# GpSimd's wide products and subtractions, cut into pieces of 256 or 288 columns

## The chip, the core and the metric

The kernel runs on one core of a Trainium2 chip. Five engines work side by side, each through a queue of its own that it takes in order: TensorE (PE in the profile, its weight loads PEld), VectorE (DVE), ScalarE (ACT), GpSimd (POOL) and SyncE (SP), which here issues the DMAs. They wait for one another by semaphores. The metric is the device time of one execution in microseconds (us).

## The reference

Attention with a top-32 mask, over 8 batches, 8 heads, 576 positions and a head size of 64, and then a gated feed-forward network on its output (4608 rows of 512, inner size 1536), all in float32:

```python
scores = scale * np.matmul(q, k.transpose(0, 1, 3, 2))
kth = np.partition(scores, -top_k, axis=-1)[..., -top_k:-top_k + 1]
scores = np.where(scores >= kth, scores, -1000000000.0)
scores = scores - np.max(scores, axis=-1, keepdims=True)
attn = np.exp(scores)
attn = attn / (np.sum(attn, axis=-1, keepdims=True) + 1e-09)
attn_out = np.matmul(attn, v)
...
gate = 1.0 / (1.0 + np.exp(-(x @ w_gate)))
val = x @ w_val
return (gate * val @ w_out).astype(np.float32)
```

The 32nd largest of each row of 576 scores has to be found exactly, for 8 x 8 x 576 rows.

## The kernel before

**Attention.** A step takes one pair of heads of one batch and 128 query positions; it holds J = 2 score tiles of 128 x 576 (one for each head). The last 64 positions of a batch go in a step with J = 1, both heads sharing one tile. There are 8 x 4 x 5 = 160 steps, 288 tiles in all. The five position blocks of a batch are worked in two groups, blocks 0 and 1, then 2 to 4.

A step goes through three passes, which lie one step apart in program order. `load_queries` (L172) and `load_keys` (L155) bring operands. Each float32 operand is split in a rounded part, made by ScalarE, and the rest, made by GpSimd by a subtraction (L163 for the keys, on 64 of the 128 partitions, 576 columns). `scores` (L180) multiplies on TensorE and ScalarE copies the result to the tile `s` (L202).

`select` (L243) finds the threshold. VectorE takes the 8 largest of each of 8 segments (`cand`, L262) and from them the 8th to the 24th largest in rounds (L266, L268). With a bound a little above the 24th, ScalarE writes the sign of every score against the bound to `under`, in bfloat16, and counts (L274, one instruction for each tile). GpSimd then writes u = s x under for both tiles (L277), VectorE takes the 8 largest of u (`below`, L281, one for each tile), and L282 picks the wanted one into `kths`. Meanwhile ScalarE forms the exponentials `e` (L209). In `masked` (L211) VectorE multiplies e by the mask s >= kth and sums (L214, inputs `s` and `e`); GpSimd and VectorE form the reciprocal (L217, L218, L220). In the pass after, `turn` transposes `e` on TensorE (L301) and `weigh` multiplies it by the values; GpSimd writes the rest of that product too (`xl`, L344).

**Feed-forward.** `ffn` (L346) is a generator: for each group of 256 or 320 rows it makes three products for each weight tile (L377 to L379), the gate (L382 to L385, GpSimd writes `gl` in L385) and three products with the second weights (L397 to L399), summed up by GpSimd (L405). `run` (L410) draws pieces of it between the steps of attention, some 384 rows behind.

**Weights.** `split_weight` (L115) takes each of 18 weight blocks, in two halves of 512 columns, from its float64 words to two float32 parts. VectorE works on the bit patterns (L138 to L140), GpSimd multiplies `frac` by `lead` (L142), TensorE adds the parts up (L145 to L147). Nine blocks are split during the first group's steps, the others at their first use, all in the first 336 us of the profile.

**What sets the order.** The instructions are written in program order, and the framework lays down each engine's queue and the semaphores by a planner that forecasts the time of every instruction (`schedule_with_timeline_sim=True`). At run time each engine follows its own queue in order. Dependencies go by the part of a tile that an instruction reads or writes.

Of the kernel before, what the change touches and what calls it, by code (L numbers as in the profile page):

```python
# [10 lines left out]
F32 = mybir.dt.float32  # L11
# [5 lines left out]
ALU = mybir.AluOpType  # L17
# [11 lines left out]
def tile_topk_attention_then_gated_ffn(  # L29
# [8 lines left out]
    nc = tc.nc  # L38
    P = 128
    B, H, _, S = k.shape  # L40
    D = P // 2
    HALF = S // 2
# [72 lines left out]
    def split_weight(idx, held):  # L115

        if held:
            wt = pools["w"].tile([P, 2, 2, NP, P], F32R, tag="w", name=f"wsplit_{idx}")
            ready[idx] = wt
        for i in range(2):
            raw = pre_pools["raw"].tile([P, NP * P, 2], U32, tag="raw", name=f"wraw_{idx}_{i}")
            half = slice(i * NP * P, (i + 1) * NP * P)
            nc.sync.dma_start(raw.rearrange("p n t -> p (n t)"), w[idx][:, half].bitcast(U32))
            low, top = raw[:, :, 0], raw[:, :, 1]
            if held:
                pair = wt[:, i].rearrange("p a c n -> p a (c n)")  # L130
            else:
                pair = pre_pools["parts"].tile([P, 2, NP * P], F32R, tag="pair", name=f"wpair_{idx}_{i}")
            lead = pre_pools["parts"].tile([P, NP * P], F32, tag="lead", name=f"wt_lead_{idx}_{i}")
            rest = ps_f.tile([P, NP * P], F32, tag="f", name=f"wrest_{idx}_{i}")
            frac = pre_pools["parts"].tile([P, NP * P], F32R, tag="frac", name=f"wt_frac_{idx}_{i}")
            lead_u = lead.bitcast(U32)
            nc.scalar.activation(lead, top.bitcast(F32), AF.Copy, scale=2.0**-112)
            nc.vector.tensor_scalar(lead_u, lead_u, 3, None, op0=ALU.logical_shift_left)  # L138
            nc.vector.scalar_tensor_tensor(top, top, 0x80000000, lead_u, op0=ALU.bitwise_and, op1=ALU.bitwise_or)
            nc.vector.tensor_scalar(lead_u, top, 0xFF800000, None, op0=ALU.bitwise_and)  # L140
            nc.scalar.activation(frac, low, AF.Copy)
            nc.gpsimd.tensor_tensor(frac, frac.bitcast(F32), lead, op=ALU.mult)  # L142
            bits = top.bitcast(F32)
            nc.scalar.activation(pair[:, 0], bits, AF.Copy)
            nc.tensor.matmul(rest, ident, bits, start=True, stop=False)  # L145
            nc.tensor.matmul(rest, minus, pair[:, 0], start=False, stop=False)
            nc.tensor.matmul(rest, plus, frac, start=False, stop=True)  # L147
            nc.scalar.activation(pair[:, 1], rest, AF.Copy)
            nc.sync.dma_start(w_split[idx][:, i], pair.bitcast(F32))
# [5 lines left out]
    def load_keys(b, p, nm):  # L155

        ks = []
        for h in (2 * p, 2 * p + 1):
            raw = bkr.tile([P, S], F32, tag="kraw", name=f"kraw_{nm}_{h}")
            nc.sync.dma_start(raw, k[b, h])  # L160
            kt = bk.tile([P, S], F32R, tag="k", name=f"k_{nm}_{h}")
            nc.scalar.activation(kt, raw, AF.Copy)
            nc.gpsimd.tensor_tensor(kt[D:], raw[D:], kt[D:], op=ALU.subtract)  # L163
            ks.append(kt)
        return ks

# [40 lines left out]
    def numerators(J, s, st, e):  # L207
        for j in range(J):
            nc.scalar.activation(e[:, j], s[:, j], AF.Exp, bias=st[:, j : j + 1], scale=1.0 / SHRINK)  # L209

    def masked(J, s, kth, st, e, nm):  # L211

        for j in range(J):
            nc.vector.scalar_tensor_tensor(  # L214
                e[:, j], s[:, j], kth[j], e[:, j], op0=ALU.is_ge, op1=ALU.mult, accum_out=st[:, 4 + j : 5 + j]
            )
        nc.gpsimd.tensor_scalar(st[:, 4 : 4 + J], st[:, 4 : 4 + J], 1e-9, None, op0=ALU.add)  # L217
        nc.vector.reciprocal(st[:, 6 : 6 + J], st[:, 4 : 4 + J])  # L218
        inv = bi.tile([P, P], F32, tag="inv", name=f"inv_{nm}")
        nc.gpsimd.tensor_copy(  # L220
            inv.rearrange("p (j d) -> p j d", j=J), st[:, 6 : 6 + J].unsqueeze(2).to_broadcast([P, J, P // J])
        )
        return e, inv
# [19 lines left out]
    def select(J, s, col, nm):  # L243

        cand = b2.tile([P, 2, NSEG * 8], F32, tag="cand", name=f"cand_{nm}")
        tops = b2.tile([P, 2, 16], F32, tag="tops", name=f"tops_{nm}")
        below = b2.tile([P, 2, 8], F32, tag="below", name=f"below_{nm}")
        st = bi.tile([P, 8], F32, tag="st", name=f"st_{nm}")
        sums = bi.tile([P, 2], F32, tag="sums", name=f"sums_{nm}")
        pick = b2.tile([P, 2, 8], F32, tag="pick", name=f"pick_{nm}")
        e = b3.tile([P, 2, S], F32, tag="e", name=f"e_{nm}")
        u = b2.tile([P, 2, S], F32, tag="u", name=f"u_{nm}")
        under = b2.tile([P, 2, S], BF16, tag="under", name=f"under_{nm}")
        for j in range(J):  # L260
            for g in range(NSEG):
                nc.vector.max(cand[:, j, 8 * g : 8 * g + 8], s[:, j, g * SEG : (g + 1) * SEG])  # L262
        for r in range(LEAD // 8):
            for j in range(J):
                t = tops[:, j, 8 * r : 8 * r + 8] if r < 2 else leads[:, n_tiles - col - j : n_tiles - col - j + 8]
                nc.vector.max(t, cand[:, j])  # L266
                if r < LEAD // 8 - 1:
                    nc.vector.match_replace(cand[:, j], t, cand[:, j], LOWEST)  # L268
            if r == 0:
                nc.gpsimd.tensor_scalar(st[:, 0:J], tops[:, :J, 0], -1.0 / SHRINK, None, op0=ALU.mult)  # L270
        for j in range(J):
            at = 2 * (n_tiles - col - j + 7) + 1
            bound = leads.bitcast(BF16)[:, at : at + 1]
            nc.scalar.activation(  # L274
                under[:, j], s[:, j], AF.Sign, bias=bound, scale=-CUT, accum_out=sums[:, j : j + 1]
            )
        nc.gpsimd.tensor_tensor(u[:, :J], s[:, :J], under[:, :J], op=ALU.mult)  # L277
        numerators(J, s, st, e)
        yield
        for j in range(J):  # L280
            nc.vector.max(below[:, j], u[:, j])  # L281
            nc.vector.scalar_tensor_tensor(  # L282
                pick[:, j],
                wanted,
                sums[:, j : j + 1],
                below[:, j],
                op0=ALU.is_equal,
                op1=ALU.mult,
                accum_out=kths[:, col + j : col + j + 1],
            )  # L290
        yield masked(J, s, [kths[:, col + j : col + j + 1] for j in range(J)], st, e, nm)
# [54 lines left out]
    def ffn(nm0, xs, t0, rows, general):  # L346
# [5 lines left out]
        def load(idx):  # L352
            if idx in ready:
                return ready.pop(idx)
            if not (general or idx in stored):
                split_weight(idx, True)
                stored.add(idx)
                return ready.pop(idx)
            wt = pools["w"].tile([P, 2, 2, NP, P], F32R, tag="w", name=f"w_{nm0}_{idx}")
            nc.sync.dma_start(wt.rearrange("p i a c n -> p i a (c n)").bitcast(F32), w_split[idx])  # L360
            return wt
# [48 lines left out]
    def run(general):  # L410
# [32 lines left out]
        for n in range(len(steps) + 2):  # L443
            if n < len(steps):
                g, p, i = steps[n]
                b, first, end = groups[g]
                m = n

                if not general and g == 0:
                    k = m * (HELD + LOADED) // (2 * NP)  # L450
                    for t in range(k, (m + 1) * (HELD + LOADED) // (2 * NP)):
                        split_weight(order[t], t < HELD)
                        stored.add(order[t])
                fetch(n + FETCH)
                ask(n + ASK)
                begin(n + AHEAD)
                J = 2 if i < NT else 1
                nm = f"{mark}{b}_{i}_{p}"
                if general:
                    parts[n] = select_any(J, staged.pop(n), nm)  # L460
                else:
                    parts[n] = select(J, staged.pop(n), col, nm)
                next(parts[n])
                col += J
# [104 lines left out]
```

## Time and profile before

| | |
|---|---|
| median of 3 runs | 1672.96 us (1672.12 to 1673.5) |
| the profiled execution's own time | 1670.51 us |
| its span | 1668.7 us |
| mean granted TensorE clock | 0.978 of full speed |
| busy: PE, DVE, ACT, POOL | 1559.4, 1383.5, 1179.0, 1103.6 us |
| GpSimd: u of two tiles (L277) | 128 instructions of 128 x 1152 |
| GpSimd: u of one tile (L277) | 32 instructions of 128 x 576 |
| GpSimd: k (L163) | 64 instructions of 64 x 576 |
| GpSimd: frac (L142) | 36 instructions of 128 x 512 |

The profile shows one execution. A row of a group reads: line, engine, operation, output <- inputs, shapes, count | busy us, mean ns of one | idle us of the engine just before them, and what ended it. A row of a wait reads: who <- whom, us in all, times, the longest. In the rows of a timeline stand start and length in us. An instruction's length is from its start on the engine to its end, so what it waits for after its semaphores are there is inside it.

### The profile page before, as it was taken

The numbers are of one execution on the slowest core, as the hardware profiler recorded it, in microseconds if no ns is written. First come the engines' busy times: TensorE is split into PE (matmuls) and PEld (weight loads), VectorE is DVE, ScalarE is ACT, GpSimd is POOL, SyncE is SP. The second block draws the span as 40 slices with busy tenths as digits, with TensorE's granted clock in tenths as the row PEclk, the third lists the DMA queues.
The fourth block names the chain that finished last, engine by engine and source line by source line (L and its number), as shares of the span: only waits on it lengthen the run. The fifth ranks groups of instructions, "written<-read, shape, count | busy, mean of one in ns | idle before, by whom it ended". The sixth has DMA issues, their size and how long they took to land.

```text
span 1668.7 us, 37046 instructions
## 1 busy us (share of the span) xinstructions
PE 1559.4 (93%) x11666; PEld 1415.2 (85%) x11666; DVE 1383.5 (83%) x6353; ACT 1179.0 (71%) x2739; POOL 1103.6 (66%) x1331
## 2 busy tenths in 40 slices
PE   5678878899999999999999999999999999999998
PEld 2347756798999989999898989998898989999898
DVE  6999999968998889988989789988989789988310
ACT  7787878756777777766777677766777677766422
POOL 7667776866776767677666767677666767666323
PEclk8779999999999999999999999999999999999999
DMA  7556555777777677677686677677686677666686
GB/s 239 188 170 225 169 180 184 265 273 238 252 264 250 230 277 263 230 256 261 220 294 229 238 266 263 231 248 268 219 295 227 239 253 263 230 231 219 247 322 219
DMA packets 101006, 402.01 MB, mean 241 GB/s; under 512 B 11200, under 2 KB 39872, under 8 KB 65472
## 3 DMA queue, kind: packets, MB, share of 16 engines
q1 hardware_dynamic: 100800, 399.55, 68.7%
q8 instruction: 94, 1.54, 0.4%
q14 instruction: 112, 0.92, 0.2%
HBM read 371.20 MB, written 28.31 MB: 239 GB/s over the span
## 4 chain that ended last, share of the span: by engine, by line
PE 40%; DVE 24%; ACT 8%; POOL 5%; issue 3%; DMA 2%; POOLq 0%; ACTq 0%
DVE e L214 6%; PE pz L377 6%; PE pz L378 6%; PE pz L379 6%; DVE cand L262 6%; DVE below L281 4%; PE pss L195 4%; PE po L320 3%; POOL u L277 3%; PE po L397 3%; PE po L398 3%; PE po L399 3%; PE pt L301 2%; DVE pick L282 2%; ACT e L209 2%
## 5 line engine op out<-in xcount | busy, mean ns | idle before, releaser
L377 PE MATMUL pz<-xh,w 128*128 128x320 f32 (+1 forms) x1472 | 444.2, 302 | 4.4 <-DVE gf L383 2.4
L379 PE MATMUL pz<-xh,w 128*128 128x320 f32 (+1 forms) x1472 | 438.5, 298 | 0.0
L378 PE MATMUL pz<-xl,w 128*128 128x320 f32 (+1 forms) x1472 | 438.2, 298 | 0.0
L277 POOL TENSOR_TENSOR u<-s,under 128x1152 f32<-128x1152 f32 (+1 forms) x160 | 356.2, 2229 | 71.3 <-ACT under L274 54.7
L262 DVE MAX8 cand<-s 128x8 f32<-128x72 f32 x2304 | 350.5, 216 | 38.9 <-ACT s L202 38.2
L214 DVE SCALAR_TENSOR_TENSOR e<-s,kths,e 128x576 f32<-128x576 f32 x288 | 305.8, 1075 | 37.3 <-ACT e L209 37.1
L274 ACT ACTIVATE under<-s,leads 128x576 bf16<-128x576 f32 x288 | 223.3, 776 | 118.4 <-DVE leads L266 107.8
L377 PEld LDWEIGHTS pz<-xh,w 128*128 128x128 f32 x1472 | 278.7, 189 | 6.9 <-ACT gf L382 3.0
L378 PEld LDWEIGHTS pz<-xl,w 128*128 128x128 f32 x1472 | 278.9, 189 | 0.0
L379 PEld LDWEIGHTS pz<-xh,w 128*128 128x128 f32 x1472 | 278.7, 189 | 0.0
L385 POOL TENSOR_TENSOR gl<-gf,gh 128x256 fp32r<-128x256 f32 (+1 forms) x192 | 166.6, 868 | 129.0 <-ACT gh L384 126.2
L281 DVE MAX8 below<-u 128x8 f32<-128x576 f32 x288 | 205.9, 747 | 54.6 <-POOL u L277 54.4
L195 PE MATMUL pss<-k,qh 128*128 128x288 f32 (+2 forms) x672 | 204.3, 321 | 22.6 <-ACT s L202 15.5
L398 PE MATMUL po<-gl,w 128*128 128x320 f32 (+1 forms) x736 | 218.2, 301 | 0.0
L397 PE MATMUL po<-gh,w 128*128 128x320 f32 (+1 forms) x736 | 214.5, 307 | 2.6 <-ACT part L404 1.3
L399 PE MATMUL po<-gh,w 128*128 128x320 f32 (+1 forms) x736 | 215.5, 298 | 0.0
L302 ACT ACTIVATE et<-pt 128x384 f32<-128x384 f32 x384 | 181.3, 490 | 47.9 <-PE pt L301 46.8
L301 PE MATMUL pt<-ident,e 128*128 128x128 f32 x1152 | 184.2, 279 | 28.9 <-DVE e L214 24.2
L209 ACT ACTIVATE e<-s,st 128x576 f32<-128x576 f32 x288 | 209.4, 775 | 2.1 <-POOL st L270 2.1
L202 ACT ACTIVATE s<-pss 128x576 f32<-128x576 f32 x288 | 186.5, 648 | 3.3 <-PE pss L195 2.2
L195 PE MATMUL pss<-k,ql 128*128 128x288 f32 (+2 forms) x672 | 187.0, 299 | 0.3 <-POOL ql L177 0.3
L301 PEld LDWEIGHTS pt<-ident,e 128*128 128x128 f32 x1152 | 142.2, 143 | 42.5 <-DVE e L214 19.2
(102 smaller groups left out, 3543.7 us busy)
## 6 DMA issues: line engine op xcount, KB each, us to landing
w<-ws SPq DMA_DIRECT2D x276, 1024.0 KB, 5.2
v<-in_v_dram SPq DMA_DIRECT2D x64, 352.0 KB, 4.1
qraw<-in_q_dram SPq DMA_DIRECT2D x160, 128.0 KB, 3.6
kraw<-in_k_dram SPq DMA_DIRECT2D x64, 288.0 KB, 3.8
wraw<-in_w_dram SPq DMA_DIRECT2D x36, 512.0 KB, 4.0
ws<-wsplit SPq DMA_DIRECT2D x24, 512.0 KB, 4.4
ws<-wpair SPq DMA_DIRECT2D x12, 512.0 KB, 3.8
out_dram<-acc SPq DMA_DIRECT2D x32, 160.0 KB, 4.8
```

The lines of the kernel that those rows point to most:

```text
L195: nc.tensor.matmul(ps[:, half, o : o + n], x[:, h * P : (h + 1) * P], ks[h][:, k0 : k0 + n], start=t == 0, stop=t == len(todo) - 1,)
L214: nc.vector.scalar_tensor_tensor(e[:, j], s[:, j], kth[j], e[:, j], op0=ALU.is_ge, op1=ALU.mult, accum_out=st[:, 4 + j : 5 + j])
L262: nc.vector.max(cand[:, j, 8 * g : 8 * g + 8], s[:, j, g * SEG : (g + 1) * SEG])
L277: nc.gpsimd.tensor_tensor(u[:, :J], s[:, :J], under[:, :J], op=ALU.mult)
L281: nc.vector.max(below[:, j], u[:, j])
L301: nc.tensor.transpose(pt[:, c], ef[:, k0 : k0 + P], ident)
L377: nc.tensor.matmul(ps, wt[:, u, 0, d], xh[:, cols], start=d == 0, stop=False)
L378: nc.tensor.matmul(ps, wt[:, u, 0, d], xl[:, cols], start=False, stop=False)
L379: nc.tensor.matmul(ps, wt[:, u, 1, d], xh[:, cols], start=False, stop=d == NP - 1)
L397: nc.tensor.matmul(ps, wt[:, e % 2, 0, f], gh, start=f == 0, stop=False)
L398: nc.tensor.matmul(ps, wt[:, e % 2, 0, f], gl, start=False, stop=False)
L399: nc.tensor.matmul(ps, wt[:, e % 2, 1, f], gh, start=False, stop=f == FG - 1)
```

## The change

Three GpSimd lines are cut along the columns. `frac` goes in two pieces of 256 columns, the keys' rest in two of 288, and u in two pieces of 288 for each tile, so four instructions in place of one where J = 2. The pieces of u stand in order of the tile; each reads one half of one tile of `s` and `under`. Every product and difference is the same as before, and nothing else is changed.

```diff
@@ split_weight
-            nc.gpsimd.tensor_tensor(frac, frac.bitcast(F32), lead, op=ALU.mult)
+            for c in (slice(0, 2 * P), slice(2 * P, 4 * P)):
+                nc.gpsimd.tensor_tensor(frac[:, c], frac[:, c].bitcast(F32), lead[:, c], op=ALU.mult)
@@ load_keys
-            nc.gpsimd.tensor_tensor(kt[D:], raw[D:], kt[D:], op=ALU.subtract)
+            for c in (slice(0, HALF), slice(HALF, S)):
+                nc.gpsimd.tensor_tensor(kt[D:, c], raw[D:, c], kt[D:, c], op=ALU.subtract)
@@ select
-        nc.gpsimd.tensor_tensor(u[:, :J], s[:, :J], under[:, :J], op=ALU.mult)
+        for j in range(J):
+            for half in range(2):
+                c = slice(half * HALF, (half + 1) * HALF)
+                nc.gpsimd.tensor_tensor(u[:, j, c], s[:, j, c], under[:, j, c], op=ALU.mult)
```

## The prediction

> **What bounds the kernel now.** I read the page's totals and the chain of waits first, then the busy time by stretches, and after that who waits for whom in the stretches that stand out.
>
> ```profile
> span 1668.7 us, 37046 instructions
> PE 1559.4 (93%) x11666; PEld 1415.2 (85%) x11666; DVE 1383.5 (83%) x6353; ACT 1179.0 (71%) x2739; POOL 1103.6 (66%) x1331
> PE 40%; DVE 24%; ACT 8%; POOL 5%; issue 3%; DMA 2%; POOLq 0%; ACTq 0%
> DVE e L214 6%; PE pz L377 6%; PE pz L378 6%; PE pz L379 6%; DVE cand L262 6%; DVE below L281 4%; PE pss L195 4%; PE po L320 3%; POOL u L277 3%; PE po L397 3%; PE po L398 3%; PE po L399 3%; PE pt L301 2%; DVE pick L282 2%; ACT e L209 2%
> 0.00:84.00 84.00, 47.13 (x164) 28.94 (x165) 69.55 (x289) 66.71 (x133) 56.26 (x66) 0.79 0.64 212
> 84.00:336.00 252.00, 208.16 (x1336) 164.37 (x1335) 247.65 (x1033) 203.24 (x449) 181.53 (x196) 0.93 0.60 200
> 336.00:1540.00 1204.00, 1183.61 (x9259) 1106.40 (x9258) 1039.93 (x4938) 867.63 (x2056) 826.98 (x1016) 1.00 0.71 249
> ```
>
> A row of stretches gives the length, then busy us of PE, PEld, DVE, ACT and POOL. There are two regimes. From 84 to 336 DVE is busy 247.65 of 252 us (98%) and PE 208.16 (83%): VectorE sets the pace while the weights are split. From 336 to 1540 PE is busy 1183.61 of 1204 us, so at most 20.4 us are to be had there by feeding PE better, and DVE (86%) has room. Who PE waits for before 336 says the same:
>
> ```profile
> PE wrest L145 <- DVE wraw L139: 25.8, 12, 6.9
> PE pt L301 <- DVE e L214: 24.2, 10, 4.7
> ```
>
> **How GpSimd enters.** No row shows PE waiting long for GpSimd. It enters through VectorE, as this stretch does, one row for each instruction (start us, length us):
>
> ```profile
> 898.60 1.44 POOL L163 TENSOR_TENSOR k<-kraw,k 64x576 fp32r<-64x576 f32 x1
> 900.11 2.78 POOL L277 TENSOR_TENSOR u<-s,under 128x1152 f32<-128x1152 f32 x1
> ...
> 898.64 2.01 DVE L214 SCALAR_TENSOR_TENSOR e<-s,kths,e 128x576 f32<-128x576 f32 x1
> 900.72 2.79 DVE L214 SCALAR_TENSOR_TENSOR e<-s,kths,e 128x576 f32<-128x576 f32 x1
> ```
>
> The same instruction can take 0.79 us (row of L214 below). Here the first one starts 0.04 us after k and ends at 900.65, that is 0.61 after k's end; taking off its own 0.79, it was let go 0.18 us before k ended. The second starts during u and ends at 903.51, again 0.62 after u's end at 902.89. So this DVE instruction stands inside its own row until the running GpSimd instruction is nearly over. Between k and u the first DVE instruction got its turn, although u started 0.07 us after k; u paid with 2.78 us. Minimum, median and maximum of the lines whose rows spread like that:
>
> ```profile
> L214 DVE SCALAR_TENSOR_TENSOR e<-s,kths,e x288: 790/814/2927, 27.0 to 1554.2; 128x576 f32<-128x576 f32 x144
> L282 DVE SCALAR_TENSOR_TENSOR pick<-wanted,sums,below x288: 198/222/2404, 25.5 to 1553.8; 128x8 f32<-128x8 f32 x144
> L139 DVE SCALAR_TENSOR_TENSOR wraw<-wraw,wt_lead x36: 665/683/2916, 11.0 to 302.7; 128x512 uint32<-128x512 uint32 x36
> L138 DVE TENSOR_SCALAR wt_lead<-wt_lead x36: 397/415/1951, 10.5 to 301.3; 128x512 uint32<-128x512 uint32 x36
> L140 DVE TENSOR_SCALAR wt_lead<-wraw x36: 400/416/1758, 12.1 to 305.2; 128x512 uint32<-128x512 uint32 x36
> ```
>
> Their means before 336 us (ns, ahead of the last bar):
>
> ```profile
> L214 DVE SCALAR_TENSOR_TENSOR e<-s,kths,e 128x576 f32<-128x576 f32 x55 | 55.2, 1021 | 0.0
> L139 DVE SCALAR_TENSOR_TENSOR wraw<-wraw,wt_lead 128x512 uint32<-128x512 uint32 x36 | 38.1, 1058 | 0.0
> L282 DVE SCALAR_TENSOR_TENSOR pick<-wanted,sums,below 128x8 f32<-128x8 f32 x56 | 32.1, 592 | 0.0
> L138 DVE TENSOR_SCALAR wt_lead<-wt_lead 128x512 uint32<-128x512 uint32 x36 | 22.7, 631 | 11.4 <-ACT wt_lead L137 11.3
> L140 DVE TENSOR_SCALAR wt_lead<-wraw 128x512 uint32<-128x512 uint32 x36 | 19.5, 541 | 0.0
> ```
>
> Mean less minimum, times the count, before 336: L214 55 x 0.231 = 12.7; L282 56 x 0.394 = 22.1; L139 36 x 0.393 = 14.1; L138 36 x 0.234 = 8.4; L140 36 x 0.141 = 5.1. That is 62.4 us of standing still in the stage that VectorE bounds. Set against the GpSimd instruction that runs then, one by one, 42 of these stalls with 44.9 us lie behind the three lines that the change cuts: u 19 with 29.5 us, k 9 with 6.8, frac 14 with 8.6. The first and the last of the 42:
>
> ```profile
> 12.93 1.24 DVE L138 TENSOR_SCALAR wt_lead<-wt_lead 128x512 uint32<-128x512 uint32 x1
> ...
> 333.10 1.31 DVE L282 SCALAR_TENSOR_TENSOR pick<-wanted,sums,below 128x8 f32<-128x8 f32 x1
> ```
>
> **The change, part by part.** *GpSimd's own time.* These are the means by shape:
>
> ```profile
> L277 POOL TENSOR_TENSOR u<-s,under 128x1152 f32<-128x1152 f32 x128 | 312.5, 2445 | 57.0 <-ACT under L274 45.2 <-DMA w<-ws 2.6 <-ACT et L302 2.6
> L163 POOL TENSOR_TENSOR k<-kraw,k 64x576 fp32r<-64x576 f32 x64 | 97.1, 1518 | 23.3 <-issue 8.0 <-PE pss L195 3.9 <-DMA kraw<-in_k_dram 3.4
> L385 POOL TENSOR_TENSOR gl<-gf,gh 128x320 fp32r<-128x320 f32 x96 | 87.4, 911 | 85.8 <-ACT gh L384 85.0
> L385 POOL TENSOR_TENSOR gl<-gf,gh 128x256 fp32r<-128x256 f32 x96 | 79.1, 824 | 43.2 <-ACT gh L384 41.2 <-PE pt L301 0.6
> L142 POOL TENSOR_TENSOR wt_frac<-wt_frac,wt_lead 128x512 fp32r<-128x512 f32 x36 | 48.9, 1359 | 14.8 <-DVE wt_lead L140 11.0 <-DVE pick L282 1.4 <-DVE tops L266 1.1
> L277 POOL TENSOR_TENSOR u<-s,under 128x576 f32<-128x576 f32 x32 | 43.8, 1367 | 14.3 <-ACT under L274 9.4 <-PE pss L195 4.0 <-DMA w<-ws 0.6
> ```
>
> No row has 288 columns. The line through the two u rows (1367 at 576, 2445 at 1152) gives 289 ns + 1.87 ns a column, so 828 ns for 288 and 768 for 256; the 256 and 320 rows give 868 between them, and 824 for 256. The first pair is the lower bound, the second the upper, and I take the upper, as its shapes are nearest. u of two tiles: 4 x 868 - 2445 = +1.03 us, 128 times, 131 us (lower bound 111). u of one: 2 x 868 - 1367 = +0.37, 32 times, 12 (9). k: 2 x 868 - 1518 = +0.22, 64 times, 14 (9). frac: 2 x 824 - 1359 = +0.29, 36 times, 10 (6). Together +167 us (136), so GpSimd goes from 66% to 76%. Before 336 it is 31 u (25 of two tiles, by the 128 to 32 of the whole), 18 k and 36 frac: 26 + 2 + 4 + 10 = 42 us on top of 56.26 + 181.53, or 280 of 336 us, 83%. GpSimd does not become the bound in either regime, so I cost this part at nothing; its cover is VectorE's queue before 336 and PE's after it.
>
> *VectorE's stalls before 336.* A piece holds VectorE up for its length less 0.18, about 0.62 to 0.69 us, against 2.2 for u. If a DVE instruction arrives at any moment of a piece, it waits 0.31 to 0.34: 42 x 0.33 = 14 us remain and 31 are saved. That is the upper bound, for there is a row that speaks for more meetings:
>
> ```profile
> 332.23 0.94 DVE L282 SCALAR_TENSOR_TENSOR pick<-wanted,sums,below 128x8 f32<-128x8 f32 x1
> ...
> 332.25 0.90 POOL L385 TENSOR_TENSOR gl<-gf,gh 128x320 fp32r<-128x320 f32 x1
> 333.10 1.28 POOL L277 TENSOR_TENSOR u<-s,under 128x576 f32<-128x576 f32 x1
> ```
>
> This pick stood behind gl, and the next one (333.10, above) behind the u that followed. With pieces each DVE instruction of a pair can meet one. If all do, the second waits a piece less the 0.16 us that it needs to arrive, about 0.48: 42 x (0.33 + 0.48) = 34 us remain and 11 are saved. I take 21, half way, since L214 and L282 do come in pairs, and L138 to L140 do not. Saved DVE time becomes time where DVE is full, which is 252 of the 336 us: 21 x 0.75 = 16 us, bounds 8 and 23. Against it stands a u that ends later, which would delay L281; before 336 L281 waits for u only three times, so I take off 2: -14 us.
>
> *After 336.* Stalls shrink there as well, but PE is full, so the gain is at most the 20.4 us that PE idles. A row that speaks for some of it:
>
> ```profile
> 466.22 0.78 ACT L274 ACTIVATE under<-s,leads 128x576 bf16<-128x576 f32 x1 [2.79 <-DVE leads L266]
> 469.30 2.39 POOL L277 TENSOR_TENSOR u<-s,under 128x1152 f32<-128x1152 f32 x1 [0.21 <-ACT xh L343]
> ```
>
> The first tile's sign was ready at 467.00, and u began at 469.30, because the one instruction needs both tiles. Pieces of the first tile could start up to 2.3 us earlier, and the first L281 with them. Against it: all four end about 1 us later once they run, and what is behind them in GpSimd's queue (gl for PE's second product, acc for ACT, ql and k for the next scores) comes that much later. Bounds -20 and +15, the latter being a u longer by 1.0 us at the places where u stands on the chain (3% of 1668.7 is 50 us, some 20 of them at 2.4), less a little. I take -3.
>
> Sum, against the profiled execution's 1670.5 us: -14 - 3 gives 1653.5; the median of the runs shown, 1672.96, is 2.5 above that execution, so 1656.
>
> **The rivals.** *PE takes back its idle time too (0.12):* the earlier start of the first tile's pieces ends ACT's and PE's small waits after 336; -14 - 18 gives 1641. For it: the 2.3 us above. Against it: PE's waits there are spread over many causes.
>
> *No difference (0.13):* the pairs meet two pieces each, 11 us saved, 8 of them on the path, and the later ends of u take 8 back after 336: 1673. For it: the pair at 332.23. Against it: u's stalls are long and few, and a wait that is cut in four seldom doubles.
>
> *Slower, through u itself (0.17):* every DVE turn that falls between two pieces also holds u up, as 2.78 against a mean of 2445 ns shows (+0.3). With two turns u ends 1.0 + 0.6 us later, and L281 waits for it in order, with L262 and L214 queued behind it:
>
> ```profile
> DVE below L281 <- POOL u L277: 51.9, 47, 2.9
> ```
>
> These 47 waits of 336 to 1540 would grow by 1.6 us, 75 us of DVE's 164 idle; at the 20 places on the chain it is 32 us. Less 14 before 336 it gives 1673 + 18 = 1691, and 1675 at half as many places. It decides from the point where the later end outweighs the earlier start.
>
> *Slower, because VectorE gets no turn between the pieces (0.05):* then a stall lasts to the end of the last piece, and stalls grow with the square of the length: u (3.47 / 2.445) squared is 2.0, +30 us before 336; k and frac +2 and +4; times 0.75, +27, so 1700. The row at 898.64 speaks against it: VectorE got in between k and u. The Trainium skill, GPSIMD Engine Reference, section Instruction dispatch, says that consecutive Pool instructions are no barrier: each of the eight cores goes on to the next one as soon as its own share is done. By that rule the engine might never be free between two pieces; this trace, with the turn taken at 900.04, does not bear it out.
>
> **How the numbers follow.** The forecast, 1656, has 0.53; its own range, from 23 saved and 6 more after 336 down to 8 saved and 4 lost, is 1644 to 1669. About 0.2% (3.3 us) is what a measurement of this kernel tells from no change. Faster: 0.53 + 0.12 = 0.65. Same: 0.13. Slower: 0.17 + 0.05 = 0.22. The range takes in the first rival and most of the slower one: 1638 to 1686. What no row prices is the planner: it lays down each engine's order from its own forecast of times, and other durations can reorder any queue.
>
> **What would show it.** In the profile after: L214, L282 and L139 with maxima near 1.5 us instead of 2.9 and means closer to their minima; DVE busy about 1320 instead of 1383 us; GpSimd 1240 to 1270 us with pieces of 0.8 to 0.9; the DVE-bound stage over some 14 us sooner. It is wrong if DVE's stalls keep their sum while their number doubles, if L281's wait for u grows past 80 us, or if PE shows idle stretches after 336 with GpSimd ahead of them.

## The result, and the profile after

The changed kernel takes 1640.03 us (median of 6 runs, 1639.24 to 1640.95), the kernel before 1672.16 beside it. The ratio is 0.9813, with a 95% interval of 0.9803 to 0.9824: 32 us faster, where 17 were forecast.

The totals of the changed kernel's page with its chain of waits, and its busy time by stretches (length, then busy us of PE, PEld, DVE, ACT and POOL; the stretches are cut where the same stages end):

```profile
span 1637.9 us, 37664 instructions
PE 1560.0 (95%) x11666; PEld 1418.4 (87%) x11666; DVE 1363.1 (83%) x6353; ACT 1182.3 (72%) x2739; POOL 1200.0 (73%) x1847
PE 68%; DVE 14%; POOL 5%; ACT 3%; DMA 2%; issue 2%; POOLq 0%; ACTq 0%; SPq 0%; DVEq 0%
```

```profile
0.00:84.00 84.00, 52.41 (x188) 30.69 (x188) 71.72 (x288) 68.62 (x138) 67.67 (x104) 0.83 0.69 223
84.00:330.00 246.00, 210.17 (x1317) 165.16 (x1316) 235.97 (x1035) 203.91 (x447) 208.87 (x298) 0.91 0.59 199
330.00:1510.00 1180.00, 1176.64 (x9247) 1106.23 (x9246) 1031.07 (x4944) 868.54 (x2056) 884.87 (x1392) 1.00 0.72 255
1510.00:1638.00 128.00, 120.76 (x920) 116.32 (x918) 24.29 (x88) 41.18 (x101) 38.56 (x56) 0.99 0.73 264
```

PE's busy time is the same (1560.0 us, 1559.4 before), so the gain is PE's idle time. Before it was idle 80.7 us up to 336, 20.4 from there to 1540 and 8.2 after; now, up to 330, to 1510 and after, 67.4, 3.4 and 7.1. The splitting stage gave 13.3 us and the long middle stage 17.0. The chain of waits shows it too: DVE's share falls from 24% to 14%, and PE's rises from 40% to 68%.

The three cut lines and two of the lines that stood behind them (minimum, median and maximum in the last rows):

```profile
L282 POOL TENSOR_TENSOR u<-s,under 128x288 f32<-128x288 f32 x576 | 443.5, 792 | 104.8 <-ACT under L276 92.4 <-PE po L333 2.0 <-PE po L404 1.0
L165 POOL TENSOR_TENSOR k<-kraw,k 64x288 fp32r<-64x288 f32 x128 | 111.0, 887 | 18.8 <-POOL u L282 7.9 <-ACT k L163 3.5 <-issue 2.6
L143 POOL TENSOR_TENSOR wt_frac<-wt_frac,wt_lead 128x256 fp32r<-128x256 f32 x72 | 60.4, 858 | 14.8 <-DVE wt_lead L140 6.7 <-DVE cand L264 3.8 <-DVE tops L268 2.9
```

```profile
L216 DVE SCALAR_TENSOR_TENSOR e<-s,kths,e x288: 792/819/1509, 27.7 to 1524.9; 128x576 f32<-128x576 f32 x144
L287 DVE SCALAR_TENSOR_TENSOR pick<-wanted,sums,below x288: 197/352/835, 26.0 to 1524.5; 128x8 f32<-128x8 f32 x144
L139 DVE SCALAR_TENSOR_TENSOR wraw<-wraw,wt_lead x36: 666/892/1245, 9.9 to 297.9; 128x512 uint32<-128x512 uint32 x36
```

(L216 and L287 are L214 and L282 of before.) The longest stalls are gone: L216's maximum is 1.51 us instead of 2.93, that of the pick 0.84 instead of 2.40. But the medians of the pick and of L139 rose, from 222 to 352 and from 683 to 892 ns: stalls are shorter and more frequent.

Below, a *stall* is what L214, L282 and L138 to L140 take above their undisturbed 0.796, 0.208, 0.404, 0.670 and 0.404 us, summed over all of them; shorter ones count as nothing. These lengths are those that the shortest fifth of each line's rows stays under before. It is 178 us before and 133 in the changed kernel.

### The profile page after: what moved, and what is told of

Read it like the earlier page. It is cut to its first block, busy times and chain, and to the rows that moved or that the text cites. A ratio compares the mean times of both kernels' runs of the same rounds, so it can differ in the third digit from the quotient of the medians.

```text
span 1637.9 us, 37664 instructions
## 1 busy us (share of the span) xinstructions
PE 1560.0 (95%) x11666; PEld 1418.4 (87%) x11666; DVE 1363.1 (83%) x6353; ACT 1182.3 (72%) x2739; POOL 1200.0 (73%) x1847
## 4 chain that ended last, share of the span: by engine, by line
PE 68%; DVE 14%; POOL 5%; ACT 3%; DMA 2%; issue 2%; POOLq 0%; ACTq 0%; SPq 0%; DVEq 0%
PE pz L382 11%; PE pz L383 11%; PE pz L384 11%; PE pss L197 7%; PE po L402 5%; PE pt L306 5%; PE po L403 5%; PE po L404 5%; PE po L325 5%; DVE cand L264 3%; DVE e L216 3%; DVE below L286 2%; PE po L327 2%; DMA w<-ws 1%; POOL u L282 1%
## 5 line engine op out<-in xcount | busy, mean ns | idle before, releaser
L282 POOL TENSOR_TENSOR u<-s,under 128x288 f32<-128x288 f32 x576 | 443.5, 792 | 104.8 <-ACT under L276 92.4
L383 PE MATMUL pz<-xl,w 128*128 128x320 f32 (+1 forms) x1472 | 437.1, 297 | 0.0
L264 DVE MAX8 cand<-s 128x8 f32<-128x72 f32 x2304 | 345.1, 216 | 28.7 <-ACT s L204 27.7
L276 ACT ACTIVATE under<-s,leads 128x576 bf16<-128x576 f32 x288 | 224.4, 779 | 116.8 <-DVE leads L268 104.4
L216 DVE SCALAR_TENSOR_TENSOR e<-s,kths,e 128x576 f32<-128x576 f32 x288 | 274.0, 957 | 9.8 <-ACT e L211 7.9
L383 PEld LDWEIGHTS pz<-xl,w 128*128 128x128 f32 x1472 | 279.0, 190 | 0.1
L286 DVE MAX8 below<-u 128x8 f32<-128x576 f32 x288 | 216.6, 752 | 58.1 <-POOL u L282 56.4
L306 PE MATMUL pt<-ident,e 128*128 128x128 f32 x1152 | 179.6, 279 | 13.3 <-DVE e L216 10.3
```

The source lines that it names most:

```text
L216: nc.vector.scalar_tensor_tensor(e[:, j], s[:, j], kth[j], e[:, j], op0=ALU.is_ge, op1=ALU.mult, accum_out=st[:, 4 + j : 5 + j])
L282: nc.gpsimd.tensor_tensor(u[:, j, c], s[:, j, c], under[:, j, c], op=ALU.mult)
L306: nc.tensor.transpose(pt[:, c], ef[:, k0 : k0 + P], ident)
L383: nc.tensor.matmul(ps, wt[:, u, 0, d], xl[:, cols], start=False, stop=False)
```

## The experiments

All ratios are against runs of the kernel before on the same chip. There are three theories of the gain. *Stalls*: shorter pieces hold VectorE for less time. *Early start*: the first tile's pieces can start before the second tile's sign is there. *Planner*: it forecasts other times for the pieces and lays the queues in another order. The programs show that it does: of the instructions that run (a fall-back path does not), 24% of TensorE's stand elsewhere than before, 32% of VectorE's, 38% of ScalarE's and 29% of GpSimd's other than the cut ones (all that are not in the longest common order).

**Which part, and which property of it.** The edits are written out as loops here; the runs have the same pieces. First u alone.

```diff
-        nc.gpsimd.tensor_tensor(u[:, :J], s[:, :J], under[:, :J], op=ALU.mult)
+        for j in range(J):
+            for c in (slice(0, 288), slice(288, 576)):
+                nc.gpsimd.tensor_tensor(u[:, j, c], s[:, j, c], under[:, j, c], op=ALU.mult)
```

> Only u is cut (four pieces of 288 for two tiles, two for one); k and frac stay whole. Three theories of the 32 us. Stalls: the gain is VectorE standing for less time behind GpSimd, and u has 80 of the 113 us that lay behind the three cut lines before: about 1648 us. Early start: the gain is that pieces of the first tile run before the second tile's sign is there, which only u has: about 1640. Planner: the gain is another order of the queues: no value follows, anything from 1640 to 1680.

Measured: 1635.49 us, ratio 0.9778 (0.9761 to 0.9794). That is the whole gain, and by the ratios 0.35% more than the change; the planner laid an order of its own for this kernel too. Then k and frac alone, as the change has them:

```diff
-            nc.gpsimd.tensor_tensor(frac, frac.bitcast(F32), lead, op=ALU.mult)
+            for c in (slice(0, 2 * P), slice(2 * P, 4 * P)):
+                nc.gpsimd.tensor_tensor(frac[:, c], frac[:, c].bitcast(F32), lead[:, c], op=ALU.mult)
-            nc.gpsimd.tensor_tensor(kt[D:], raw[D:], kt[D:], op=ALU.subtract)
+            for c in (slice(0, HALF), slice(HALF, S)):
+                nc.gpsimd.tensor_tensor(kt[D:, c], raw[D:, c], kt[D:, c], op=ALU.subtract)
```

> Only k and frac are cut in two; u stays one instruction. Stalls: 33 of the 113 us lay behind k and frac, and half of the saving is in the stage that VectorE bounds: about 1662 us. Early start: nothing of it is in k and frac: 1672. Planner: no value follows; a time below 1655 or above 1680 would speak for it.

Measured: 1663.65 us, 0.9951 (0.9935 to 0.9968), as the stalls had it, though this order too is another than before. The two parts do not add up: 37 and 8 us alone, 32 together.

u by tile only, 576 columns each:

```diff
-        nc.gpsimd.tensor_tensor(u[:, :J], s[:, :J], under[:, :J], op=ALU.mult)
+        for j in range(J):
+            nc.gpsimd.tensor_tensor(u[:, j], s[:, j], under[:, j], op=ALU.mult)
```

> u is cut by tile alone: one instruction of 576 columns for each tile (about 1.29 us), k and frac stay whole. Stalls: VectorE is held up to 1.1 us instead of 2.2, so half of u's stall saving: about 1660 us. Early start: nearly all of the gain of u_only, within 4 us of it, about 1642. Planner: no relation.

Measured: 1669.33 us, 0.9984 (0.9975 to 0.9994). Pieces that can start early bring next to nothing in the order laid for them, and both forecasts, 1660 and 1642, were missed. Stalls rose, to 201 us, though each piece can hold VectorE for 1.1 us only, which the stall theory did not have.

Short pieces that cannot start early, for they cross both tiles:

```diff
-        nc.gpsimd.tensor_tensor(u[:, :J], s[:, :J], under[:, :J], op=ALU.mult)
+        for c in range(0, S, 288 // J):
+            w = slice(c, c + 288 // J)
+            nc.gpsimd.tensor_tensor(u[:, :J, w], s[:, :J, w], under[:, :J, w], op=ALU.mult)
```

> u is cut in four pieces of 144 columns of both tiles (288 elements each, as long as those of the change), so that every piece needs both signs and none can start early; with one tile two pieces of 288. k and frac stay whole. Stalls: as u_only, about 1648 us. Early start: no gain, and a u that ends 1 us later: 1672 to 1680. Planner: no relation.

Measured: 1643.86 us, 0.9838 (0.9822 to 0.9854). Most of the gain comes without the early start, so that theory is out as its main cause; whether it has a part in the 0.6% by which u alone is faster is not shown. Short pieces and a new order are still together here.

**Order and length, taken apart.** The planner's forecast depends on how many pieces there are and on their columns in all, so pieces of other widths can leave its order as it is. In the next two kernels every instruction stands at the same place as in its counterpart, on every engine, but for three pairs of neighbours that are swapped in the first of them. First the change itself with long pieces:

```diff
-            for half in range(2):
-                c = slice(half * HALF, (half + 1) * HALF)
+            for c in (slice(0, 8), slice(8, S)):
```

> The change with the pieces of u at other places: for each tile 8 columns and then 568, in place of 288 and 288; k and frac in two pieces as in the change. All queues then hold the same instructions in the same order as the changed kernel; only GpSimd's two long pieces hold VectorE for about 1.1 us instead of 0.62. Stalls: most of u's gain goes, about 1660 us. Planner: the order is that of the change, so 1640, within 4 us. Early start: the same as the change, 1640.

Measured: 1645.68 us, 0.9845 (0.9828 to 0.9863), 5 us or 0.3% slower than the change. The forecast of the stall theory, 1660, was wrong: halving the hold from 1.1 to 0.62 us is worth some 5 us in this order. The cost of the pieces is no reason, as these rows of GpSimd show (0.24 + 1.31 us against 2 x 0.79):

```profile
L277 POOL TENSOR_TENSOR u<-s,under 128x568 f32<-128x568 f32 x288 | 377.9, 1312 | 0.1
...
L277 POOL TENSOR_TENSOR u<-s,under 128x8 f32<-128x8 f32 x288 | 69.7, 242 | 105.0 <-ACT under L274 95.0 <-PE po L328 2.0 <-DMA w<-ws 0.3
```

Then the pieces across both tiles, with a last one about as long as the u of before:

```diff
-        for c in range(0, S, 288 // J):
-            w = slice(c, c + 288 // J)
+        for w in (slice(0, 8), slice(8, 16), slice(16, 24), slice(24, S)):   # J = 1: 0 to 8, 8 to S
```

> The counterpart: the queues of the run with four pieces of both tiles (144 columns of each), every instruction at the same place, but the pieces are 8, 8, 8 and 552 columns of both tiles, so the last holds VectorE for nearly as long as the u of before (about 2.1 us). Stalls: back to 1665 or more. Planner: within 5 us of the 1643.9 of the even pieces.

Measured: 1670.55 us, 1.0000 (0.9991 to 1.0009). All of the gain is gone in the very order that had it. So this order alone brings no time; long holds undo it. The stalls are 177 us, as before the change (129 with the even pieces).

Now the other way round: the queues of before as they were laid, and u cut afterwards at its place (the edit in words):

```diff
+    # after the planner: each u in GpSimd's queue becomes 4 instructions of 288 columns (2 for one tile);
+    # the first waits for what u waited for, the last signals what u signalled
```

> The kernel before with its queues exactly as the planner laid them for it, and each u then replaced, at its place, by four pieces of 288 columns (two for one tile); the first piece waits for what u waited for, the last one signals. No other instruction stands elsewhere. Stalls: the pieces alone bring the gain of u, about 1645 us. Planner: the pieces alone bring nothing, and GpSimd's added 0.8 us for each u costs a little: 1670 to 1680. Both in parts: between.

Measured: 1677.39 us, 1.0036 (1.0022 to 1.0049): slower. So the pieces alone do not bring the gain either. The profile says why. First the two stalled lines of this run as groups (mean ns ahead of the last bar), then VectorE's waits in it (us in all, times, longest):

```profile
L214 DVE SCALAR_TENSOR_TENSOR e<-s,kths,e 128x576 f32<-128x576 f32 x288 | 290.3, 1022 | 41.5 <-ACT e L209 41.3
L282 DVE SCALAR_TENSOR_TENSOR pick<-wanted,sums,below 128x8 f32<-128x8 f32 x288 | 111.0, 400 | 0.3
```

```profile
DVE below L281 <- POOL u L277: 91.4, 87, 3.3
...
DVE e L214 <- ACT e L209: 41.3, 31, 4.0
```

The same waits of the kernel before, and then of the changed one:

```profile
DVE below L281 <- POOL u L277: 54.4, 50, 2.9
...
DVE e L214 <- ACT e L209: 37.1, 28, 4.0
```

```profile
DVE below L286 <- POOL u L282: 56.4, 91, 2.1
...
DVE e L216 <- ACT e L211: 7.9, 19, 0.9
```

In the old order the pieces cut VectorE's stalls from 178 to 139 us, and its wait for u grew from 54 to 91: what one gives the other takes. In the order of the change the wait for u does not grow, though its pieces are as long, and that for `e` nearly goes.

One more thing differs between this run and the change: in the old order the first piece waits for both signs and only the last one signals, while in the change each L286 needs the pieces of its own tile alone. The first L286 of a step with two tiles starts before the last piece has ended in 127 of 128 steps of the change, and in none of this run. The run with the crossing pieces settles that this is not what the gain needs: there too no L281 starts before the last piece, there are as many pieces of as many elements, and k and frac are whole. Only the order differs, and it stands at 0.9838 against 1.0036, with a wait for u of 55 us against 91.

With k and frac cut in place too:

```diff
+    # as above, and each k and each frac becomes two instructions of half the columns
```

> As the run before it, with k and frac replaced in place by two pieces each as well, so that GpSimd does exactly the pieces of the change in the order of before. Stalls: about 1640 us, the time of the change. Planner: 1670 to 1685.

Measured: 1686.26 us, 1.0087 (1.0073 to 1.0101). GpSimd does all the pieces of the change here, and the kernel is 46 us slower than the change. VectorE waits 105 us for u.

Last, half as many pieces in the old order (in words again, against the run with four):

```diff
-    # each u of two tiles becomes 4 instructions of 288 columns
+    # each u of two tiles becomes 2 instructions of 576 columns; u of one tile stays whole
```

> The queues of before once more, with each u of two tiles replaced in place by two pieces of 576 columns; u of one tile stays whole. The four pieces in this order cut VectorE's stalls by 38 us and made its wait for u 30 us longer. If the one is given back by the other, two pieces, which hold VectorE for 1.1 instead of 2.2 us and make u only 0.2 us longer, should keep part of the gain: stalls down by some 20 us, the wait for u up by less than 10, and 1660 to 1668 us. If VectorE's stalls do not count in this order whatever u does: 1672 to 1677.

Measured: 1671.42 us, 0.9996 (0.9987 to 1.0005), no difference. The value expected from half the stalls, 1660 to 1668, was missed, and the time lies just below the other, 1672 to 1677: stalls fell by 8 us and not by 20, and the wait for u rose by 12 to 66.3.

**The queues in program order, and more pieces.** The two kernels with the planner's forecast switched off, which keeps their orders more alike (of the instructions that run, 2% of TensorE's, 16% of VectorE's, 7% of ScalarE's and 4% of GpSimd's uncut ones stand elsewhere; the shares in the expectation count a fall-back path too, which does not run):

```diff
-    with tile.TileContext(nc, schedule_with_timeline_sim=True) as tc:
+    with tile.TileContext(nc, schedule_with_timeline_sim=False) as tc:
```

> The kernel before, with the planner laying the queues by the program's order instead of by forecast times. It only serves as the base of the next run; some per cent slower or faster than 1672 us, no theory says which.

> The changed kernel, its queues laid by the program's order as in the run before it; the two have nearly the same order on every engine (1% of TensorE's instructions, 10% of VectorE's and GpSimd's stand elsewhere). Stalls: 1 to 2% faster than its base. Planner: within 0.3% of its base.

Measured: 1929.68 and 1949.36 us, 1.1545 and 1.1669 of the kernel before, so the pieces cost 1.1% there. Both forecasts, 1 to 2% faster and within 0.3%, were missed. The stalls are 78 us in the first and 74 in the second: there was little to save in that order, and VectorE's wait for `e` rose from 19 to 55 us. That the pieces cost time fits the run in the old order, though this regime, where VectorE waits some 300 us for u in both, is far from the kernel's.

u alone, in pieces of 144 columns:

```diff
-            for c in (slice(0, 288), slice(288, 576)):
+            for c in (slice(0, 144), slice(144, 288), slice(288, 432), slice(432, 576)):
```

> u in pieces of 144 columns, eight for two tiles and four for one; k and frac whole. Stalls alone: each piece holds VectorE for some 0.3 us instead of 0.62, so the stalls behind u halve again; PE is nearly full already, so 1630 to 1636 us against 1635.5 of the four pieces. If GpSimd's own time decides by then (each piece has a fixed part, so u of two tiles takes about 4 us instead of 3.2): above 1645.

Measured: 1647.1 us, 0.9840 (0.9823 to 0.9856), by the ratios 0.6% or 10 us behind the pieces of 288, where 1630 to 1636 was the forecast of the stalls alone. Stalls fall further, to 127 us, but u of two tiles now takes 8 x 0.52 = 4.2 us, and the wait for it is 77 us. That is the other forecast, above 1645: GpSimd's time decides by then, and the wait for u is where it shows.

**All of them in one table.** us, from each profiled execution; VectorE's waits are those for u (L281) and for `e` (L214).

| kernel | ratio | stalls | wait for u | wait for e | sum | span |
|---|---|---|---|---|---|---|
| before | 1 | 178 | 54 | 37 | 270 | 1668.7 |
| the change | 0.9813 | 133 | 56 | 8 | 197 | 1637.9 |
| u alone | 0.9778 | 141 | 53 | 10 | 204 | 1635.7 |
| u, crossing pieces | 0.9838 | 129 | 55 | 17 | 201 | 1641.4 |
| the change, 8 + 568 | 0.9845 | 140 | 53 | 9 | 202 | 1642.5 |
| u, 144 columns | 0.9840 | 127 | 77 | 15 | 219 | 1645.7 |
| k and frac alone | 0.9951 | 163 | 52 | 25 | 241 | 1662.0 |
| crossing, 8 + 8 + 8 + 552 | 1.0000 | 177 | 52 | 14 | 242 | 1667.8 |
| u by tile | 0.9984 | 201 | 55 | 8 | 264 | 1667.0 |
| old order, u in 2 | 0.9996 | 170 | 66 | 36 | 272 | 1670.3 |
| old order, u in 4 | 1.0036 | 139 | 91 | 41 | 272 | 1679.0 |
| old order, all pieces | 1.0087 | 134 | 105 | 42 | 281 | 1684.4 |
| program order, before | 1.1545 | 78 | 307 | 19 | 403 | 1925.5 |
| program order, the change | 1.1669 | 74 | 289 | 55 | 418 | 1944.9 |

Stalls alone do not order these kernels (139 us stands at 1679.0 and 140 at 1642.5). The sum of the three nearly does: five kernels with 197 to 219 us lie between 1636 and 1646, the next seven, with 241 to 281, between 1662 and 1684, and the two in program order, with 403 and 418, far behind. Inside the seven it tells less: 242 and 270 stand at nearly the same time. It is lost time of VectorE, whether it stands in an instruction or ahead of one. VectorE has the same work in all of these kernels, so the sum is in part bookkeeping: it tells where the time went, and the runs with the order held tell why.

## Why the prediction was right or wrong

**The direction and the number.** 1656 was forecast and 1640 measured, inside the range; the rival "PE takes back its idle time too", at 1641 with a chance of 0.12, gave the number. Its reason, the early start, is not what the gain needs (0.9838 without it), so its number was in good part luck. The 2.3 us that it rested on were not free either: from 467.65 to 469.08 GpSimd worked on ql and gl, so in the order of before no piece could have started much sooner.

**Before 336: -14 forecast, 13.3 measured, by a poorer way than the one worked out.** The step took 21 us of stalls off. Up to 336 all stalls went from 61 to 49 us, 12 us. Those behind the three cut lines went only from 44.9 to 39.7, in 108 places instead of 42. The pairs met more pieces than even the lower bound (11 us saved) allowed, and the rest of the fall is behind lines that were not cut, ql above all (8.8 to 3.8 us): shorter pieces of the cut lines do not explain that, another order may. With the order of before held and all pieces cut, the stalls behind the same three lines went from 44.9 to about 32 us, in 84 places: 13 us saved, close to the lower bound and to its reason, that every stall meets two pieces. PE's idle time up to 336 fell there by 5.4 us only, from 80.7 to 75.3. So the low end of this step was right, the 21 taken was too much, and more than half of the 13.3 us is not there without the new order. The sign that the stage would be over some 14 us sooner did not come: the last L139 starts at 297.9 instead of 302.7 us. What came in its place is work that PE had done by then, 262.6 us up to 330 against 255.3 up to 336. The sum was right and its working was not.

**After 336: -3 forecast, 17.0 measured.** This is the step that failed in size. Its bound, the 20.4 us that PE idled, was right, and the choice of 3 was not: 3.4 us of idle time are left. I reasoned that PE was full and that later pieces would push GpSimd's queue back. In fact VectorE's lost time reaches PE there too, by way of ScalarE. The first row is PE's longest wait from 336 to 1500 before, the second ScalarE's wait for the bound that `under` needs, in the whole kernel before:

```profile
PE pss L195 <- ACT s L202: 10.4, 17, 1.1
ACT under L274 <- DVE leads L266: 107.8, 76, 3.2
```

Of the 20.4 us that PE idles in that stretch before, 19 end on a row of ScalarE, and going back along ScalarE's queue from these rows, its last idle time was ended by VectorE (L266, L383 or L337) in all but 0.3 us of them. In the change the first of the two waits is 0.6 us (the second, of the whole kernel, 104.4). These rows show the stretch from 336 to 1500 in the kernel with u in four pieces in the old order, where PE idles 24.6 of 1164 us, and in the change, where it idles 3.4.

```profile
336.00:1500.00 1164.00, 1139.43 (x8862) 1063.34 (x8862) 975.17 (x4744) 828.30 (x1972) 855.32 (x1290) 1.00 0.70 249
```

```profile
336.00:1500.00 1164.00, 1160.64 (x9122) 1092.22 (x9122) 1018.32 (x4878) 859.37 (x2032) 873.67 (x1371) 1.00 0.73 255
```

**What no step had: the planner.** The prediction named it as unpriced and left it in the width of the range. It is a condition of the whole gain. With the order of before the same pieces cost 0.9%, and those of u alone 0.4%; with a new order and holds as long as before nothing is gained. It takes both. Why the new orders cover the longer u is open. With the crossing pieces the planner has moved what waits for u away from it: in VectorE's queue the first L281 of a step stands 21 instructions behind the step's last L266 for a bound (the median), and 17.5 before. In the change it stands only 2 behind, nearer than before, but needs only its own tile's pieces. Open is also why the order laid for u by tile, a smaller step in the same direction, has more stalls and not fewer.

**The slower rival "through u itself" was a true mechanism.** Where the order was held, L281's wait for u grew by 37 us and the kernel became 0.4% slower, 1677, near the 1675 that this rival gave for half the places. In the change itself the wait stayed at 56.4, under the 80 that was to show the prediction wrong.

**VectorE gets its turn between pieces.** The last rival, that it would not, is refuted by rows like these of the changed kernel: two pieces back to back, and an L216 that starts in the first and ends 0.60 us before the second does.

```profile
883.16 2.52 POOL L282 TENSOR_TENSOR u<-s,under 128x288 f32<-128x288 f32 x2
...
883.80 1.28 DVE L216 SCALAR_TENSOR_TENSOR e<-s,kths,e 128x576 f32<-128x576 f32 x1
```

The pair takes 2.52 us here, instead of 1.44 for an undisturbed pair of the same kernel (at 876.97). The page GPSIMD Engine Reference of the Trainium skill, section Instruction dispatch, lets a core go on to the next instruction before the others have finished; no run shows that this keeps VectorE out.

**GpSimd's time was overrated.** +136 to +167 us were forecast and 96 measured (1103.6 to 1200.0): a piece of u takes 792 ns in the mean, not 828 to 868, and some of GpSimd's other lines became shorter. The rows it was taken from were means that held stalls of their own. DVE's busy time fell to 1363 us and not to 1320: the stalls fell by 45 us only, its other rows grew by 7, and 18 us less of its rows overlap, which leaves 20.

## What to carry to other kernels

In this kernel a long GpSimd instruction makes some VectorE instructions stand until it is nearly over, so its length is a cost on VectorE, not only on GpSimd; pieces shorten each stall but lengthen the result's delay, and here only orders that the planner laid for pieces kept the difference, not all of them. Where a planner lays the queues, test such an edit with the order held and with the order alone, as here, before the gain is put down to the edit. Cut first what holds the critical engine longest: u alone did as well as cutting everything (by the ratios 0.35% better, in an order of its own), and twice as many pieces were worse.

## What the runs showed of the hardware

The fixed part of a GpSimd product is near 0.2 us, an estimate: u takes 0.24 us at 8 columns (mean above). An 8-column DVE pick with two inputs in SBUF stands behind GpSimd as long as a 576-column L214 does: the longest take 2.2 and 2.1 us above their undisturbed lengths before, 0.6 and 0.7 after. Shorter holds raise the number of stalls, so their sum falls less than their length: with the order held and u cut in four, the longest stall falls from 2.2 to 1.2 us, and the stalls behind u go from some 75 to some 130 in the whole kernel while their sum goes from 80 to 49 us.
